# First couple's scores in two parts, joined sums and a newly laid order in a kernel of attention, gated MLP and mixture attention

## The chip, the cores and the metric

One core of a Trainium2 chip runs the whole program. The metric is the device time of one execution in microseconds (us), the median of several runs. The engines are named TensorE (PE in the rows, PEld its weight loads), VectorE (DVE), ScalarE (ACT), GpSimd (POOL) and SyncE (SP, which issues DMAs).

## The reference

Three layers follow one another, on 4 batches of 576 positions and 512 channels.

```python
# first attention: 8 heads of 64, each position sees itself and the 63 before it
scores = scale * np.matmul(q, k.transpose(0, 1, 3, 2))
scores = np.where((rel >= 0) & (rel < 64), scores, -1e9)
attn = np.exp(scores - np.max(scores, axis=-1, keepdims=True))
attn = attn / (np.sum(attn, axis=-1, keepdims=True) + 1e-09)
x = attn @ v
# gated MLP
h = np.maximum(x @ w_in, 0.0); u, v = h[..., :512], h[..., 512:]
v_n = (v - mean(v)) / np.sqrt(var(v) + 1e-06)
x = (u * (np.einsum('ts,bsd->btd', w_spatial, v_n) + b_spatial)) @ w_out
# second attention: 4 experts, causal over 576 positions, the two best by x @ w_gate
for e in range(4):
    a = softmax(scale * (x @ wq[e]) @ (x @ wk[e]).T, causal)   # sum + 1e-09
    out += gate_weight[e] * (a @ (x @ wv[e]) @ wo[e])
```

## The kernel before

The three layers run as one stream of small pieces of work. Each piece is a node (a call of `N`, with the engine that does it, what it depends on, the buffers it takes and gives back). The table `ORDER` near the head of the file lists the nodes' numbers in the order in which their instructions are written out, and the string `ON` the engine of each node that may go to several (0 PE, 1 ACT, 2 DVE, 3 POOL, 4 SP). So the order on every engine is fixed when the program is built; an engine works through its own queue in that order and waits only where a semaphore makes it. Class `Planner`, whose method `start` keeps a clock for each engine, holds the rules by which such a table is found; its `CLASH` (VectorE against GpSimd) and `cold` (TensorE after a pause) are part of it. None of the planner runs on the chip.

The work falls into three stages that overlap.

*First attention* (`a_couple`, about 0 to 110 us). A group is a pair of heads with 192 query positions; two groups make a couple, and 24 couples are worked one after another. For a couple, TensorE computes 12 score blocks of 64 queries by 128 keys into two PSUM banks, one for each head of the pairs (`s_mm`, issued by the helper at L400); VectorE adds the mask, takes the row's bound and writes SBUF (`s_top`, L647, three instructions for each bank, each with a short one that reads its accumulator); ScalarE takes the exponential and the row sum (`s_exp`, L654, three for each bank); VectorE adds the prepared 1e-9 and takes the reciprocal (L673 and L675 on a tile `mx` for each bank); one of POOL, DVE and ACT scales (`s_norm`, L663); TensorE transposes (L681); and a copy `pt` (L411 on ACT, L415 on DVE) makes the operand of the product with v. The couples from `N_DT` = 16 on ("far") are transposed by VectorE (L702) and through DRAM instead; there both banks share one tile `mp`, with one reduction and one reciprocal (L698, L700).

The first two couples (n0 = 0 and 2) read their q and k from one load each, `kq`, of 768 columns. Ahead of the first scores TensorE multiplies a tile of zeros, `hot`: `WARM` such matmuls in one node, and single ones that the order puts where it likes.

*Gated MLP* (about 20 to 260 us). Weights and x are split into a high and a low part (names ending in h and l), and each product is three matmuls. TensorE's matmuls `bank<-xh,w`, `bank<-w,xl`, `bank<-wsp_h,vh` belong here. Copies and subtractions that make the parts are the helpers at L411, L413, L415 (copy on ACT, POOL, DVE) and L424 (subtract).

*Second attention* (about 240 to the end). `c_qk` and `c_v` make q, k and v of two experts at a time, `c_gate` the gate, `far`, `far4` and `unit` the scores, exponentials, sums plus 1e-9 and scaling (L1641 to L1656, L1686 to L1699, L1725 to L1732), `c_pv` the product with v, `c_wo` the output product, whose copies `ot` SyncE stores. A block of output is 128 positions by 512 columns; for the last batch's second block it is two halves of 256.

The lines that matter most:

```python
    a = N((PE, 427.0 * WARM), lambda e: heat(WARM), alloc=[warm], prio=-1e9)      # L518
    dve.tensor_tensor_reduce(out=at(j, e2), in0=sq(ps[:, j * 128:(j + 1) * 128]),  # s_top
                             in1=sq(mask(j)), scale=-0.125, scalar=3.0e38,
                             op0=ALU.add, op1=ALU.min, accum_out=mx[:, j, 0:1])
    act.activation(at(j, e2), at(j, e2), AF.Exp, bias=mx[:, j, 0:1], scale=-1.0,   # s_exp
                   accum_out=mx[:, j, 1:2])
    dve.tensor_reduce(out=mx[:, :, 3], in_=mx[:, :, 1:3], axis=AX.X, op=ALU.add)   # L673
    dve.reciprocal(mx[:, :, 3], mx[:, :, 3])                                       # L675
```

Of the kernel before, what the change touches and what calls it, by code (L numbers as in the profile page):

```python
# [1926 lines left out]
```

## Time and profile before

| | |
|---|---|
| runs | 407.94, 409.22, 411.59 us; median 409.22 |
| profiled execution | 408.59 us, of which the span of the trace is 406.8 |
| TensorE busy | 390.8 us (96%), granted clock 0.998 on average |
| VectorE, ScalarE, GpSimd busy | 333.2, 208.8, 209.9 us |
| moved by DMA | 72.45 MB |

The times are those of one core. The span runs from the first to the last instruction of the trace; durations and stretches below count from its start. TensorE's matmuls overlap in their records, so that a full stretch shows as all busy. A matmul in full 32-bit precision leaves two records.

### The profile page before, as it was taken

The page shows a single profiled execution, that of the slowest core. Times are in us where ns is not written, and L with a number is a line of the kernel's source. Part 1 is how long each engine was busy: PE and PEld are TensorE (multiplying, and loading weights), DVE is VectorE, ACT ScalarE, POOL GpSimd, SP SyncE. Part 2 cuts the span into 40 slices and gives each one's busy share as a digit, 9 for nine tenths or more (in the row PEclk, how much of TensorE's full clock was granted, in tenths as well). Part 3 has the DMA queues.
Part 4 walks back from the last instruction along what each step waited for, and adds up shares of the span by engine and source line. Part 5 has one row for each costly group of instructions (what it writes and reads, how often), then busy time and mean ns, then how long its engine had stood idle before and what let it go on. Part 6 is the DMA issues. An engine that isn't in the chain of part 4 may idle for free.

```text
span 406.8 us, 10676 instructions
## 1 busy us (share of the span) xinstructions
PE 390.8 (96%) x3678; PEld 346.3 (85%) x3678; DVE 333.2 (82%) x1213; ACT 208.8 (51%) x708; POOL 209.9 (52%) x278
## 2 busy tenths in 40 slices
PE   8798898999999999999999999999899989999996
PEld 7676688998799989998999999999689968896765
DVE  5998799879889868758747685899999999998852
ACT  4999786955296574321222141483573346354332
POOL 7787697455279545526371765355742255122400
PEclk9999999999999999999999999999999999999999
DMA  7999769679695855450220110028775977899874
GB/s 270 290 348 314 236 157 302 202 217 271 174 341 150 235 151 155 121 161 12 76 75 3 26 54 2 1 45 230 190 180 128 263 166 210 250 278 252 234 225 129
DMA packets 88410, 72.45 MB, mean 178 GB/s; under 512 B 15138, under 2 KB 80418, under 8 KB 88356
## 3 DMA queue, kind: packets, MB, share of 16 engines
q1 hardware_dynamic: 88356, 71.77, 61.3%
q8 instruction: 29, 0.48, 0.5%
q14 instruction: 25, 0.20, 0.1%
HBM read 47.89 MB, written 23.86 MB: 176 GB/s over the span
## 4 chain that ended last, share of the span: by engine, by line
PE 64%; DVE 23%; DMA 6%; ACT 3%; issue 3%; SPq 1%; POOL 0%; DVEq 0%; ACTq 0%
PE bank L400 63%; DVE p L1641 2%; DVE pa L647 2%; DVE p L1656 2%; DVE p L1686 2%; ACT pa L654 1%; DVE qk L424 1%; DMA qa<-in_qT_dram 1%; DMA d<-p 1%; SPq L506 1%; DMA pg<-d 1%; DMA kt<-in_kT_dram 1%; DMA dr<-pa 1%; DVE p L1653 1%; DVE pa L702 1%
## 5 line engine op out<-in xcount | busy, mean ns | idle before, releaser
L400 PE MATMUL bank<-xh,w 128*128 128x288 f32 x512 | 106.8, 296 | 0.4 <-DVE xl L424 0.4
L400 PEld LDWEIGHTS bank<-xh,w 128*128 128x128 f32 x512 | 83.5, 188 | 2.2 <-DVE xl L424 0.7
L400 PE MATMUL bank<-xl,w 128*128 128x288 f32 x256 | 75.4, 294 | 0.0
L400 PE MATMUL bank<-w,xh 128*128 128x512 f32 (+1 forms) x256 | 64.6, 342 | 0.1
L1653 POOL TENSOR_SCALAR p<-p,mg,fx 128x256 f32<-128x256 f32 (+3 forms) x45 | 27.7, 624 | 42.6 <-DVE ga L1539 10.0
L400 PEld LDWEIGHTS bank<-xl,w 128*128 128x128 f32 x256 | 48.1, 188 | 0.4
L400 PEld LDWEIGHTS bank<-w,xh 128*128 128x128 f32 x256 | 42.7, 188 | 5.2 <-ACT xh L411 0.3
L400 PE MATMUL bank<-w,xl 128*128 128x512 f32 (+1 forms) x128 | 43.3, 338 | 0.9 <-DVE xl L424 0.9
L1645 ACT ACTIVATE p<-p,mg 128x128 f32<-128x128 f32 (+3 forms) x56 | 30.9, 553 | 18.9 <-DVE mg L1641 10.6
L654 ACT ACTIVATE pa<-pa,mp 128x128 f32<-128x128 f32 x96 | 37.2, 391 | 2.2 <-issue 2.0
L647 DVE CUSTOM_DVE_ANT_0 pa<-bank,mask 128x128 f32<-128x128 f32 x120 | 28.4, 283 | 4.2 <-PE bank L400 4.1
L400 PE MATMUL bank<-qk 64*128 64x320 f32 (+4 forms) x288 | 27.7, 329 | 2.5 <-DVE qk L424 2.0
L400 PEld LDWEIGHTS bank<-qk 64*128 64x128 f32 x288 | 22.0, 185 | 6.8 <-ACT xh L411 1.8
L400 PEld LDWEIGHTS bank<-w,xl 128*128 128x128 f32 x128 | 24.1, 188 | 4.0 <-DVE xl L424 1.3
L1072 POOL TENSOR_TENSOR st<-st,nhalf 128x1 f32<-128x1 f32 (+1 forms) x20 | 14.2, 715 | 24.7 <-DVE st L1070 19.3
L1641 DVE CUSTOM_DVE_ANT_0 p<-bank,kmask 128x128 f32<-128x128 f32 (+3 forms) x56 | 25.1, 482 | 0.5
L424 POOL TENSOR_TENSOR vl<-vr,vh 128x512 fp32r<-128x512 f32 x14 | 19.2, 1374 | 11.0 <-ACT vh L411 10.7
L400 PE MATMUL bank<-pg,v 128*64 128x128 f32 (+2 forms) x224 | 23.9, 354 | 1.0 <-DVE qk L424 1.0
L400 PE MATMUL bank<-wsp_h,vh 128*128 128x288 f32 x80 | 24.0, 301 | 0.3 <-DVE mp L647 0.3
L400 PE MATMUL bank<-wsp_h,vl 128*128 128x288 f32 x80 | 23.6, 295 | 0.0
L400 PE MATMUL bank<-wsp_l,vh 128*128 128x288 f32 x80 | 23.6, 294 | 0.0
L1656 DVE STREAM_TRANSPOSE p<-p 128x768 f32<-128x768 f32 (+1 forms) x21 | 22.2, 1057 | 0.9 <-POOL p L1653 0.8
(277 smaller groups left out, 1053.6 us busy)
## 6 DMA issues: line engine op xcount, KB each, us to landing
vt<-in_v_dram SPq DMA_DIRECT2D x12, 512.0 KB, 5.8
dr<-pa SPq DMA_DIRECT2D x64, 96.0 KB, 3.1
pt<-dr SPq DMA_DIRECT2D x16, 384.0 KB, 4.7
d<-p SPq DMA_DIRECT2D x56, 96.0 KB, 2.0
qa<-in_qT_dram SPq DMA_DIRECT2D x44, 96.0 KB, 5.3
out_dram<-ot SPq DMA_DIRECT2D x15, 256.0 KB, 3.6
y<-in_w_in_dram SPq DMA_DIRECT2D x7, 512.0 KB, 6.3
d<-p SPq DMA_DIRECT2D x28, 128.0 KB, 3.0
```

Of the source, the lines that this page charges most:

```text
L400: pe.matmul(o, lhsT, rhs, start=start, stop=stop)
L424: engs[e].tensor_tensor(out=o, in0=a, in1=hi.bitcast(F32), op=ALU.subtract)
L506: nc.sync.dma_start(o, i)
L647: dve.tensor_tensor_reduce(out=at(j, e2), in0=sq(ps[:, j * 128:(j + 1) * 128]), in1=sq(mask(j)), scale=-0.125, scalar=3.0e38, op0=ALU.add, ...
L654: act.activation(at(j, e2), at(j, e2), AF.Exp, bias=mx[:, j, 0:1], scale=-1.0, accum_out=mx[:, j, 1:2])
L702: a = N((DVE, 902), lambda e: dve.transpose(pa.t, pa.t), [a], use=[pa], prio=prio, sbuf=True)
L1072: a = N((POOL, 560), lambda e: pool.tensor_tensor(out=st[:m, 9:10], in0=st[:m, 8:9], in1=nhalf[:m], op=ALU.pow), [n1], use=[st])
L1641: a = N((DVE, t_tt(L)), lambda _, ps=ps, c0=c0, L=L, I=I, e=e, n=n: dve.tensor_tensor_reduce(out=put(I, e), in0=as4(ps[:, c0:c0 + L]), in1 ...
L1645: done.append(N((ACT, 284 + 0.87 * L), lambda _, I=I, e=e, n=n: act.activation(put(I, e), put(I, e), AF.Exp, bias=mg[:, n, 0:1], scale=-1. ...
L1653: done.append(N({POOL: 328 + 0.832 * L, DVE: 190 + 0.52 * L}, lambda en, n=n, I=I, e=e: engs[en].tensor_scalar(put(I, e), put(I, e), mg[:, ...
L1656: a = N((DVE, 100 + 4.16 * w), lambda e: dve.transpose(P[:, :4 * w], P[:, :4 * w]), done, use=[P], prio=prio, sbuf=True)
L1686: dve.tensor_tensor_reduce(out=P[HALF[y], i * 320:(i + 1) * 320], in0=ps[y][HALF[y], :320], in1=tmask[HALF[y], 2 * i:2 * i + 2].rearrange( ...
```

## The change

- `kq`: the first couple's q and k are laid out anew in DRAM and loaded in two parts, 384 columns and 512; the second couple's load has 896 columns.
- The first couple's scores become two nodes: 4 matmuls (j = 0), which need only the first load, and 8 (j = 1, 2). `s_top` and `s_exp` are divided in the same way.
- Joined sums: the couples n0 = 4 to 14 use the shared tile `mp`, so that one reduction and one reciprocal (L716, L718 in the new numbering) serve both banks; both scalings depend on them.
- The tiles `mc` and `mg` of the second attention's sums are made once, set to 1e-9, and kept (nine memsets on POOL); the tensor_scalar that adds the constant stays, its result in another column for `mc`.
- `WARM` 7 to 5; in all there are 13 matmuls of `hot` in place of 18.
- Planner: a VectorE instruction on SBUF waits until GpSimd is free, and the reverse, in place of `CLASH`; pauses of TensorE add up to a debt; some costs are raised.
- `ORDER` and `ON` are replaced as a whole.

Among the engines of nodes, going by the counts before and after: `v` copies on VectorE 6 to 1, `pg` copies on VectorE 4 to 1, `qk` casts on VectorE 11 to 9, scalings of `p` on VectorE by `mg` 11 to 10, `wsp_l` subtractions on VectorE 0 to 2, `xl<-y,xh` subtractions on VectorE 0 to 2, 128x192 casts `xh` on VectorE 8 to 12 and `pt` copies on VectorE 1 to 2. One scaling of the first attention in three parts goes to ScalarE.

```diff
-WARM = 7
+WARM = 5
...
 ON = (
-    "00040440020220442404012201424441212110431244230222223232202243203410012412020421102320002244142132201241100220041222433123124314"
+    "00040004000220440414444444024204411222301224122042212341201221232412401012212202230323410120422124323011402022020222241013113244"
...
-    MX = [const.tile([128, 3, 4], F32, name=f"mx{i}") for i in range(6)]
+    MX = [const.tile([128, 3, 4], F32, name=f"mx{i}") for i in range(4)]
...
-    MP = [const.tile([128, 2, 3, 4], F32, name=f"mp{i}") for i in range(3)]
-    for x in MP:
+    MP = [const.tile([128, 2, 3, 4], F32, name=f"mp{i}") for i in range(4)]
+    MC = [const.tile([128, 6], F32, name=f"mc{i}") for i in range(4)]
+    MG = [const.tile([128, 4, 4], F32, name=f"mg{i}") for i in range(5)]
+    for x in MP + MC + MG:
         pool.memset(x, 1e-9)
...
-        Q_N[2 * x] = Q_N[2 * x + 1] = KV_N["kq", x] = load(128 * 3072, 1, lambda: dma(kq(x), kq0[x]), use=[KQ[x]], prio=prio)
+        KV_N["kq", x] = []
+        for cs in (slice(0, 384), slice(384, 896)) if x == 0 else (slice(0, 896),):
+            KV_N["kq", x].append(load(512 * (cs.stop - cs.start), 1, lambda cs=cs: dma(kq(x)[:, cs], kq0[x][:, cs]), use=[KQ[x]], prio=prio))
+        Q_N[2 * x] = Q_N[2 * x + 1] = KV_N["kq", x][-1]
...
+        if n0 == 0:
+            for js in ((0,), (1, 2)):
+                tops.append(N((PE, 60 + 210 * len(js)), lambda e, js=js: s_mm(e, js), kn[:1 if js[0] == 0 else None] + tops,
+                              alloc=[] if tops else bank, use=hk + (bank if tops else []), prio=prio, form=1))
+            top = tops[-1]
...
-        if far:
+        both = far or n0 >= 4
+        if both:
             mp = r_mp.new()
         for e2, ps in enumerate(bank):
-            mx = mp if far else r_mx.new()
+            mx = mp if both else r_mx.new()
...
+        if both:
+            a = N((DVE, 90), lambda e: dve.tensor_reduce(out=mp[:, :, :, 3], in_=mp[:, :, :, 1:3], axis=AX.X, op=ALU.add),
+                  done, use=[mp], prio=prio)
+            a = N((DVE, 116), lambda e: dve.reciprocal(mp[:, :, :, 3], mp[:, :, :, 3]), [a], use=[mp], prio=prio)
+            norms = [(a, mp, x) for x in norms]
...
-    r_mc = ring(p2, "mc", [128, 6], F32, 4)
-    r_mg = ring(p2, "mg", [128, 4, 4], F32, 5)
+    r_mc, r_mg = fixed(MC, False), fixed(MG, False)
```

The head of TensorE's queue before: `hot` are the fillers, `vt` holds the first couple's q and k, banks 69 and 70 take its scores.

```order
L400 MATMUL bank_68<-hot 128x128 x9
L400 MATMUL bank_69<-vt 64x128
L400 MATMUL bank_70<-vt 64x128
L400 MATMUL bank_69<-vt 64x128
L400 MATMUL bank_70<-vt 64x128
```

The same place after:

```order
L415 MATMUL bank_68<-hot 128x128 x11
L415 MATMUL bank_69<-vt 64x128
L415 MATMUL bank_70<-vt 64x128
L415 MATMUL bank_69<-vt 64x128
L415 MATMUL bank_70<-vt 64x128
```

Eleven fillers in place of nine stand ahead of the first scores. In the whole queue there were groups of 9, 2, 3 and 4 fillers; now there are groups of 11 and 2.

VectorE's queue before, in the first couples: `mx_92` and `mx_93` belong to the two banks of the first couple, `mx_94` to the second couple, `mx_96` and `mx_97` to the third (n0 = 4); ISA is the `s_top` instruction.

```order
L647 ISA pa,mx_95<-bank_72,mask_84 128x128
L647 ISA mx_95 128x1
L673 TENSOR_REDUCE mx_92<-mx_92 128x3
L675 RECIPROCAL mx_92<-mx_92 128x3
L647 ISA pa,mx_96<-bank_73,mask_84 128x128
L647 ISA mx_96 128x1
L647 ISA pa,mx_96<-bank_73,mask_84 128x128
L647 ISA mx_96 128x1
L647 ISA pa,mx_96<-bank_73,mask_84 128x128
L647 ISA mx_96 128x1
L673 TENSOR_REDUCE mx_93<-mx_93 128x3
```

After, from the last of the first couple's six subtractions on:

```order
L676 ISA pa,mx_93<-bank_70,mask_84 128x128
L676 ISA mx_93 128x1
L711 TENSOR_REDUCE mx_92<-mx_92 128x3
L713 RECIPROCAL mx_92<-mx_92 128x3
L676 ISA pa,mx_94<-bank_71,mask_83 128x128
L676 ISA mx_94 128x1
L676 ISA pa,mx_94<-bank_71,mask_84 128x128
L676 ISA mx_94 128x1
L676 ISA pa,mx_94<-bank_71,mask_84 128x128
L676 ISA mx_94 128x1
L711 TENSOR_REDUCE mx_93<-mx_93 128x3
L676 ISA pa,mx_95<-bank_72,mask_83 128x128
```

The first couple's reductions and its first reciprocal come before and between the second couple's subtractions, where they stood behind all of them. The third couple's sums before are an L673 and an L675 for each of `mx_96` and `mx_97`; after, they are one pair on `mp_100` for both banks, in this place:

```order
L871 SCALAR_TENSOR_TENSOR y_338<-bank_70,y_338 128x512
L716 TENSOR_REDUCE mp_100<-mp_100 128x6
L676 ISA pa,mp_101<-bank_68,mask_84 128x128
L676 ISA mp_101 128x1
L676 ISA pa,mp_101<-bank_68,mask_84 128x128
L676 ISA mp_101 128x1
L676 ISA pa,mp_101<-bank_68,mask_84 128x128
L676 ISA mp_101 128x1
L718 RECIPROCAL mp_100<-mp_100 128x6
```

Its reduction comes behind the subtractions of the next couple's first bank (`mp_101`).

The end of TensorE's queue before, the output product's last blocks:

```order
L400 MATMUL bank_75<-w,oh_3477 128x512 x2
L400 MATMUL bank_75<-w,ol_3483 128x512
L400 MATMUL bank_75<-w,oh_3478 128x512 x2
L400 MATMUL bank_75<-w,ol_3484 128x512
L400 MATMUL bank_68<-w,oh_3477 128x256 x2
L400 MATMUL bank_68<-w,ol_3483 128x256
L400 MATMUL bank_68<-w,oh_3478 128x256 x2
L400 MATMUL bank_68<-w,ol_3484 128x256
L400 MATMUL bank_69<-w,oh_3477 128x256 x2
L400 MATMUL bank_69<-w,ol_3483 128x256
L400 MATMUL bank_69<-w,oh_3478 128x256 x2
L400 MATMUL bank_69<-w,ol_3484 128x256
```

And after:

```order
L415 MATMUL bank_71<-w,oh_3470 128x256 x2
L415 MATMUL bank_71<-w,ol_3476 128x256
L415 MATMUL bank_71<-w,oh_3471 128x256 x2
L415 MATMUL bank_71<-w,ol_3477 128x256
L415 MATMUL bank_75<-w,oh_3470 128x512 x2
L415 MATMUL bank_75<-w,ol_3476 128x512
L415 MATMUL bank_75<-w,oh_3471 128x512 x2
L415 MATMUL bank_75<-w,ol_3477 128x512
L415 MATMUL bank_69<-w,oh_3470 128x512 x2
L415 MATMUL bank_69<-w,ol_3476 128x512
L415 MATMUL bank_69<-w,oh_3471 128x512 x2
L415 MATMUL bank_69<-w,ol_3477 128x512
```

The two halves of 256 columns stood last; now two blocks of 512 columns follow them, the last into bank 69. On ScalarE the last copy becomes `ot<-bank_69 128x512`, where it was `128x256`; on SyncE the last output becomes one of 256 columns from a buffer that two 64x512 outputs read just before.

## Rows read from the trace of the kernel before

**Rows 1.** The page: busy time, share and instructions of each engine

```profile
PE 390.8 (96%) x3678; PEld 346.3 (85%) x3678; DVE 333.2 (82%) x1213; ACT 208.8 (51%) x708; POOL 209.9 (52%) x278
```

**Rows 2.** Stretches: us, busy PE, PEld, DVE, ACT, POOL, PEclk, DMA share, GB/s

```profile
0.00:10.00 10.00, 8.56 (x100) 7.51 (x100) 5.09 (x38) 4.29 (x17) 7.16 (x37) 1.00 0.78 267
10.00:30.00 20.00, 17.28 (x272) 13.63 (x272) 19.73 (x115) 19.65 (x84) 16.49 (x20) 1.00 1.00 325
10.00:80.00 70.00, 62.68 (x815) 52.42 (x816) 63.19 (x293) 61.03 (x242) 51.77 (x54) 1.00 0.86 264
80.00:110.00 30.00, 30.00 (x344) 25.92 (x343) 25.94 (x93) 13.86 (x53) 13.79 (x14) 1.00 0.80 233
290.00:340.00 50.00, 46.57 (x392) 40.77 (x393) 47.66 (x178) 24.85 (x76) 22.27 (x29) 1.00 0.75 191
```

**Rows 3.** TensorE in time, from 1 us: start, us, what, idle before

```profile
1.05 4.21 PE L400 MATMUL bank<-hot 128*128 128x128 f32 x18 [1.05 <-DVE hot L432]
5.19 1.28 PE L400 MATMUL bank<-vt 64*64 64x128 f32 x24
...
7.86 0.94 PE L400 MATMUL bank<-hot 128*128 128x128 f32 x6
...
10.60 1.00 PE L400 MATMUL bank<-ut,qa 64*64 64x128 f32 x24 [0.99 <-DVE mx L673]
```

**Rows 4.** VectorE in time, its first score row

```profile
6.66 0.29 DVE L647 CUSTOM_DVE_ANT_0 pa<-bank,mask 128x128 f32<-128x128 f32 x1 [3.67 <-PE bank L400]
```

**Rows 5.** Groups of VectorE, 0 to 111: busy, mean ns, idle before

```profile
L675 DVE RECIPROCAL mx<-mx 128x3 f32<-128x3 f32 x16 | 2.8, 173 | 0.2
...
L673 DVE TENSOR_REDUCE mx<-mx 128x3 f32<-128x6 f32 x16 | 2.3, 151 | 0.0
L424 DVE TENSOR_TENSOR wol<-y,woh 128x576 fp32r<-128x576 f32 x1 | 2.1, 2053 | 0.0
...
L424 DVE TENSOR_TENSOR t2w<-y,t1w 64x576 fp32r<-64x576 f32 x1 | 0.7, 742 | 0.0
```

**Rows 6.** Groups of ScalarE, 10 to 60

```profile
L654 ACT ACTIVATE pa<-pa,mx 128x128 f32<-128x128 f32 x41 | 15.9, 398 | 0.0
...
L411 ACT ACTIVATE pt<-bank 128x384 f32<-128x384 f32 x15 | 6.7, 482 | 0.4 <-PE bank L681 0.3
...
L411 ACT ACTIVATE xh<-bank 128x192 fp32r<-128x192 f32 x10 | 3.0, 329 | 3.5 <-DVE xt L415 3.3
```

**Rows 7.** GpSimd and VectorE in time, near 286 us

```profile
286.20 1.42 POOL L424 TENSOR_TENSOR xl<-y,xh 128x576 fp32r<-128x576 f32 x1
...
286.25 1.47 DVE L1539 TENSOR_TENSOR ga<-lg 128x80 f32<-128x80 f32 x1
...
287.65 0.23 DVE L1540 TENSOR_TENSOR ga<-lg 128x80 f32<-128x80 f32 x1
```

**Rows 8.** Groups of VectorE, 240 to the end

```profile
L1653 DVE TENSOR_SCALAR p<-p,mg,fx 128x128 f32<-128x128 f32 (+3 forms) x11 | 5.7, 517 | 0.1
L415 DVE CAST qk<-bank 128x288 fp32r<-128x288 f32 x11 | 4.8, 439 | 1.7 <-PE bank L400 1.6
...
L415 DVE COPY v<-bank 128x256 f32<-128x256 f32 x6 | 2.5, 417 | 1.9 <-PE bank L400 1.8
...
L415 DVE COPY pg<-bank 128x512 f32<-128x512 f32 (+2 forms) x4 | 2.3, 584 | 1.1 <-PE bank L1741 1.1
```

**Rows 9.** What TensorE waited for: us in total, times, longest

```profile
PE bank L400 <- DVE qk L424: 3.0, 4, 1.4
```

**Rows 10.** ScalarE in time, at the end

```profile
399.80 0.60 ACT L411 ACTIVATE ot<-bank 128x512 f32<-128x512 f32 x1 [6.21 <-PE bank L400]
...
403.60 0.38 ACT L411 ACTIVATE ot<-bank 128x256 f32<-128x256 f32 x1 [0.37 <-PE bank L400]
```

**Rows 11.** DMA issues, 395 to 407: count, KB each, median us to landing

```profile
out_dram<-ot SPq DMA_DIRECT2D x3, 256.0 KB, 2.1
out_dram<-ot SPq DMA_DIRECT2D x4, 128.0 KB, 1.9
```

More of the change, by code (lines that the diff above doesn't have):

```diff
@@ L253, in start @@
         n.by = e
-        if e == PE and t - self.free[e] > 1500.0:
-            self.cold = t + 3400.0
-        self.free[e] = n.end = t + n.on[e]
-        if e == PE:
-            self.free[e] = n.end = n.end + self.DRAIN[self.form][n.form] + min(n.on[e], max(0.0, self.cold - t))
+        if e == POOL:
+            t = max(t, self.claim)
+        c, d = n.on[e], self.claimed
+        idle = max(0.0, t - self.free[e])
+        self.free[e] = n.end = t + c
+        if e == PE:
+            self.debt += idle
+            if idle > 1100.0 or self.debt > 1800.0:
+                self.cold, self.debt = t + 6000.0, 0.0
+            self.free[e] = n.end = n.end + self.DRAIN[self.form][n.form] + min(c, max(0.0, self.cold - t))
+            self.debt = max(0.0, self.debt - 0.5 * (n.end - t))
             self.form = n.form
         elif e == DVE:
+            self.claimed = None
             if n.sbuf:
-                self.free[e] = n.end = n.end + self.CLASH * max(0.0, self.free[POOL] - t)
-            self.sbuf = n.sbuf
-        elif e == POOL and self.sbuf:
-            self.free[e] = n.end = n.end + self.CLASH * max(0.0, self.free[DVE] - t)
+                self.claimed, self.claim, self.queued = n, t, -1.0
+                if self.free[POOL] > t:
+                    self.queued = self.free[POOL]
+                    self.free[e] = n.end = self.queued + c
+        elif e == POOL and d is not None and self.free[DVE] > t:
+            if self.queued >= 0.0 and t <= self.queued + 60.0:
+                self.queued = n.end
+                self.free[DVE] = d.end = n.end + d.on[DVE]
+                for s in d.use:
+                    s.free_at = max(s.free_at, d.end + self.LAT[DVE])
+            else:
+                self.free[e] = n.end = self.free[DVE] + c
         if e == SP:
@@ L622, in vap, with s_mm @@
             return hv[x][:, vi, c:c + 64]
-        def s_mm(_):
-            for j in range(3):
+        def s_mm(_, js=range(3)):
+            for j in js:
                 for x, e in ((0, 0), (1, 1), (1, 0), (0, 1)):
@@ L663, in s_norm @@
                     engs[e].tensor_tensor(out=o, in0=o, in1=mx[:, :, 3:4].to_broadcast([128, 3, 128]), op=ALU.mult)
[L665 to L670 removed]
+            own_ = both and e2 == 1
+            news = ([] if own_ else [mx]) + ([] if e2 else [pa])
+            if tops:
+                for js, t in zip(((0,), (1, 2)), tops):
+                    a = N((DVE, 210 * len(js)), lambda e, js=js, s_top=s_top: s_top(e, js=js), [t] + first, alloc=news,
+                          use=[ps] + ([] if news and not e2 else [pa]) + ([] if news else [mx]), prio=prio)
+                    news, first = [], [a]
+                    a = N((ACT, 390 * len(js)), lambda e, js=js, s_exp=s_exp: s_exp(e, js=js), [a], use=[pa, mx], prio=prio)
+            else:
+                a = N((DVE, 606), s_top, [top] + first, alloc=news, use=[ps] + ([mx] if own_ else []) + ([pa] if e2 else []), prio=prio)
+                first.append(a)
+                a = N((ACT, 1160), s_exp, [a], use=[pa, mx], prio=prio)
+            if both:
                 done.append(a)
+                norms.append(s_norm)
                 continue
@@ L1546, in c_gate @@
-        n2 = N_(150, lambda: tr_(out=rk(), in_=gt(), axis=AX.X, op=ALU.add), [n2])
-        n2 = N_(80, lambda: dve.tensor_scalar(rk(), rk(), 1.5, None, op0=ALU.is_lt), [n2])
-        n2 = N_(90, lambda: tt(out=ex.t, in0=ex.t, in1=rk(), op=ALU.mult), [n2, n4])
-        n2 = N_(90, lambda: tr_(out=m1(1), in_=ex.t, axis=AX.X, op=ALU.add), [n2])
-        n2 = N_(70, lambda: dve.tensor_scalar(m1(1), m1(1), 1e-9, None, op0=ALU.add), [n2])
-        n2 = N_(75, lambda: dve.reciprocal(m1(1), m1(1)), [n2])
@@ L1552, in c_gate @@
-        n4 = N_(90, lambda: tt(out=ex.t, in0=ex.t, in1=lead(1), op=ALU.mult), [n2])
-        n4 = N_(70, lambda: dve.tensor_copy(ex[HALF[1], 4, 0:NE:2], ex[HALF[1], 4, 1:NE:2]), [n4])
+        n2 = N_(270, lambda: tt(out=gt(), in0=gt(), in1=eq(), op=ALU.add), [n2, n3])
+        n2 = N_(260, lambda: tr_(out=rk(), in_=gt(), axis=AX.X, op=ALU.add), [n2])
+        n2 = N_(160, lambda: dve.tensor_scalar(rk(), rk(), 1.5, None, op0=ALU.is_lt), [n2])
+        n2 = N_(200, lambda: tt(out=ex.t, in0=ex.t, in1=rk(), op=ALU.mult), [n2, n4])
@@ L1554, in c_gate @@
+        n2 = N_(200, lambda: tr_(out=m1(1), in_=ex.t, axis=AX.X, op=ALU.add), [n2])
+        n2 = N_(160, lambda: dve.tensor_scalar(m1(1), m1(1), 1e-9, None, op0=ALU.add), [n2])
+        n2 = N_(160, lambda: dve.reciprocal(m1(1), m1(1)), [n2])
+        n4 = N_(200, lambda: tt(out=ex.t, in0=ex.t, in1=lead(1), op=ALU.mult), [n2])
+        n4 = N_(160, lambda: dve.tensor_copy(ex[HALF[1], 4, 0:NE:2], ex[HALF[1], 4, 1:NE:2]), [n4])
         n1 = nf
```

135 lines of the change are left out of this document (67 added, 68 removed), and 126 rows, old and new, of the table ORDER.

## Prediction

> **What bounds the kernel now.** I read the page first, then the stretches, then the order of instructions at the start, the groups of the stretches in which TensorE stands still, the table of what TensorE waits for, and the end.
>
> The busy line gives TensorE 390.8 of 406.8 us (96%) and VectorE 333.2 (82%) [rows 1]. TensorE bounds the whole, and a gain has to come out of its 16.0 us without work. The stretches say where these lie [rows 2]: 10 - 8.56 = 1.44 us in 0 to 10, 70 - 62.68 = 7.32 in 10 to 80, 50 - 46.57 = 3.43 in 290 to 340, while 80 to 110 has 30.00 of 30. In 10 to 30 both helpers are full (VectorE 19.73 of 20, ScalarE 19.65); in 290 to 340 only VectorE is (47.66 of 50, ScalarE 24.85). So the early pauses are shared by two engines, and the late ones belong to VectorE.
>
> A measurement of this kernel can tell about 1% from no change: its three runs spread from 407.94 to 411.59 us. Faster therefore means under 405.1 and slower over 413.3.
>
> **The start.** TensorE begins with nine filler matmuls, 18 records in 4.21 us from 1.05, or 0.234 us a record; the first couple's scores follow at 5.19, and their row names no wait [rows 3]. So the fillers ahead of them in the queue hold them, not the load. VectorE's first subtraction starts at 6.66, having waited 3.67 us for TensorE [rows 4]. The change loads the first third apart and lets VectorE begin after 4 of the couple's 12 matmuls. But the order still puts both parts behind the fillers, and these are now eleven. Two more cost 2 x 2 x 0.234 = 0.94 us, so the scores start near 6.1; VectorE gains at most two thirds of the 24 score records, 0.67 x 1.28 = 0.85 us. They cancel: 0, between -0.9 (the two fillers add nothing) and +0.9 (the split brings nothing).
>
> **Joined sums.** Six couples (4 to 14) have one reduction and one reciprocal in place of two each. These take 151 and 173 ns [rows 5], so six couples save 6 x 0.324 = 1.9 us of VectorE, if the wider forms cost what the narrow ones do. Against that, the first head's scaling now waits for the second head's three exponentials, 3 x 0.398 = 1.2 us a couple [rows 6], and TensorE's transposes stand behind that scaling. Other moved work eats the saving: four 128x192 casts (329 ns on ScalarE) and one 128x384 copy (482 ns) go from ScalarE to VectorE. By ScalarE's rows that is 4 x 0.329 + 0.482 = 1.8 us, and ScalarE takes over one scaling in three parts, which I set at 3 x 0.398 = 1.2 us [rows 6]. VectorE comes out even (-1.9 + 1.8), ScalarE 0.6 us lighter. By the amount of work alone the 7.32 us hardly shrink; what is left is the order: the second head's sum of the first couple is taken earlier, two later blocks of fillers are gone, and each helper's queue is laid out afresh. I take a quarter of the idle time: -1.8 us. Bounds: -5.5 (three quarters go) and +2.4 (two of the six couples show their 1.2 us).
>
> **VectorE's work of the middle.** Four subtractions of 128x576 with both inputs in SBUF (two for wsp_l, two for xl) come to VectorE. One of that shape took VectorE 2.053 us (wol), one of 64 rows and the same length 0.742 [rows 5]. Four cost 3.0 to 8.2 us of VectorE. Their cover is TensorE's dense run, 80 to 110 with 30.00 of 30 for one [rows 2], so I enter 0, and +2.0 for the range if one comes just where TensorE needs VectorE next. The spread has a reason in the trace: GpSimd began a 1.42 us subtraction at 286.20, and VectorE's 128x80 comparison at 286.25 took 1.47 us, the next of that size 0.23 [rows 7].
>
> [...]
>
> **The second attention.** Here VectorE loses work [rows 8]: five of six v copies at 0.417 (2.1 us), three of four pg copies at 0.584 (1.75), two of eleven qk casts at 0.439 (0.9), one of the eleven p scalings at 0.517 (0.5); the output and oh copies cancel but for some tenths. Sum -5.2 us. The constant added to the sums costs what it did, since it was a tensor_scalar before. ScalarE takes most of the copies and has 50 - 24.85 = 25 us free in 290 to 340 [rows 2]. TensorE waits for VectorE's qk subtractions 3.0 us in four waits, the longest 1.4 [rows 9], and idles 3.43 us there. The 5.2 us are spread over 160 us, and some lie behind the last of these waits; so I take 2.0 of the 3.43. Bounds: -3.4 (all of it) and +2.0 (ScalarE's longer queue makes the qk casts, and so the subtractions, late).
>
> **The end.** Before, the last block is 256 columns wide: its copy takes 0.38 us, a 512 wide one 0.60 [rows 10], and of the outputs the 128 KB ones land 1.9 us after issue, the 256 KB ones 2.1 [rows 11]. Now the last block is 512 wide: 0.22 + 0.2 = +0.4. Behind its output SyncE issues one more, of 256 columns, out of a buffer that two 64-row outputs have to leave first. For that I add 0.3. Together +0.7, between 0 and +1.9 (that output starts only when another has landed).
>
> **Sum.** 0 - 1.8 + 0 - 2.0 + 0.7 = -3.1 us. The profiled execution took 408.59 us (its span is 406.8): 405.5. The median of the runs shown lies 0.63 higher, which gives 406.1. I put the forecast between them, at 405.7; the likeliest case's own range is 402.5 to 409.
>
> **Rivals.**
> *The pauses only move.* A new order shortens the pauses one sees and opens others where TensorE is dense today only because the helpers happen to be ahead. For it: VectorE and ScalarE together have no less to do before 80. Against: VectorE has 5.2 us less after 240. Then only the end counts: 408.6 + 0.7 = 409.3.
>
> *Most pauses go.* Beyond the start 7.32 + 3.43 = 10.75 us are idle. If the order now spares VectorE the waits behind GpSimd (1.47 us in place of 0.23), three quarters may go: 408.6 - 8.1 + 0.7 = 401.2. Against: ScalarE is full in 10 to 30 [rows 2] whatever the order.
>
> *Slower: TensorE runs at half speed after the first couple.* Before, blocks of two, three and four fillers stand among the first couples' scores; of these only the two are left. The rows show that idling has a price at the start: a filler record takes 0.234 us from 1.05 on and 0.94 / 6 = 0.157 at 7.86; 24 score records take 1.28 us at 5.19 and 1.00 at 10.60 [rows 3]. [...] If TensorE works at half speed in half of 10 to 30, 8.64 us of its 17.28 are doubled, and the idle 2.72 / 2 soak up 1.4: 405.7 + 8.6 - 1.4 = 412.9; in all of the stretch it is near 420. It decides once 3.1 + 1.4 = 4.5 us of work are doubled, for then the gain is gone. For it: the 1.2 us waits for joined sums fall in this stretch. Against: a pause of 0.99 us ahead of 10.60 left those 24 records at 1.00 [rows 3].
> [...]
>
> **How the numbers follow.** Forecast 0.47, of which 0.22 fall under 405.1 and 0.25 within 1%. The pauses only move: 0.22 (0.17 within, 0.05 slower). Most pauses go: 0.17, faster. Half speed: 0.14, slower. That makes faster 0.39, same 0.42, slower 0.19. The bounds do not all fall on one side at once, so the range takes them in part: down to 400.0, which holds most of the second rival, up to 412.8, where the half-speed case begins. About 0.06 is left out below and 0.13 above.
>
> **What would show it.** Right: the first scores near 6.1 and VectorE's first subtraction still between 6.3 and 7.0; TensorE's idle time in 10 to 80 near 5.5 us and in 290 to 340 near 1.4; VectorE some 5 us less busy after 240; a last copy of 0.60 us on ScalarE and an output issued behind it. Wrong: VectorE starting a microsecond sooner; 24 score records taking over 1.2 us after 10 (half speed); idle time of TensorE between 110 and 260; transposes that wait over 1 us for the joined sums in several couples.

## The result and the profile after

The changed kernel takes 413.06 us (median of 9 runs, 411.53 to 414.80), the kernel before 409.70 beside it (9 runs, 407.94 to 411.59): a ratio of 1.0079, with a 95% interval of 1.0052 to 1.0105. It is slower by 0.8%, and 7.4 us above the forecast of 405.7. The profiled execution took 412.33 us; its span of 410.6 is 3.8 above the 406.8 of before.

The busy line of the page answers to [rows 1]:

```profile
PE 390.9 (95%) x3668; PEld 346.6 (84%) x3668; DVE 336.6 (82%) x1211; ACT 208.2 (51%) x707; POOL 204.5 (50%) x279
```

TensorE has the same 390.9 us of work as before (390.8), so the 3.8 us are, but for 0.1, time in which TensorE stands still. Where they arose is read from the stretches, as in [rows 2] (us, busy PE, PEld, DVE, ACT, POOL, PEclk, DMA share, GB/s). The kernel after:

```profile
0.00:10.00 10.00, 8.14 (x98) 7.25 (x98) 4.77 (x31) 3.92 (x15) 7.48 (x45) 1.00 0.82 256
10.00:20.00 10.00, 7.79 (x111) 5.90 (x111) 9.46 (x58) 9.53 (x44) 5.46 (x8) 0.83 0.98 305
10.00:80.00 70.00, 62.19 (x830) 51.75 (x834) 66.30 (x293) 61.90 (x243) 49.18 (x51) 0.98 0.87 261
80.00:260.00 180.00, 175.85 (x1579) 163.76 (x1572) 140.39 (x421) 67.99 (x228) 92.18 (x108) 1.00 0.46 131
260.00:400.00 140.00, 138.28 (x1138) 118.66 (x1138) 123.38 (x467) 72.55 (x221) 55.69 (x77) 1.00 0.70 189
400.00:410.60 10.60, 6.48 (x34) 5.18 (x33) 1.78 (x4) 1.79 (x3) 0.00 (x0) 0.91 0.54 168
```

The kernel before, in the stretches that [rows 2] do not have:

```profile
80.00:260.00 180.00, 179.56 (x1630) 167.87 (x1630) 138.98 (x426) 73.26 (x238) 94.57 (x107) 1.00 0.44 128
260.00:400.00 140.00, 136.48 (x1113) 115.59 (x1113) 125.48 (x459) 68.04 (x210) 56.37 (x81) 1.00 0.72 194
400.00:406.80 6.80, 3.51 (x28) 2.89 (x24) 0.42 (x1) 2.14 (x5) 0.00 (x0) 0.90 0.50 170
```

A stretch's length less TensorE's busy time is its idle time. The difference of the two kernels stands beside the terms of the forecast:

| stretch | idle before | idle after | difference | term of the forecast |
|---|---|---|---|---|
| 0 to 10 | 1.44 | 1.86 | +0.4 | start: 0 |
| 10 to 80 | 7.32 | 7.81 | +0.5 | joined sums and order: -1.8 |
| 80 to 260 | 0.44 | 4.15 | +3.7 | VectorE's work of the middle: 0 |
| 260 to 400 | 3.52 | 1.72 | -1.8 | second attention: -2.0 |
| 400 to the end | 3.29 | 4.12 | +0.8 | end: +0.7 |

The sum is +3.6, which with 0.1 of TensorE's work is the 3.8 of the spans but for rounding. The terms miss by 0.4 + 2.3 + 3.7 + 0.2 + 0.1 = 6.7 us of the 7.4; the rest is the median of the runs, 0.7 above the profiled execution. Two lines went as forecast, and one that stood at zero decides.

The runs below that share an order in a stretch show how far one trace speaks. In 80 to 260 TensorE idles 0.00 to 0.44 us with the order of before (before, h1, h2, p, c_all, j) and 2.96 to 5.20 with that of the change (after, e1 to e5, w1), so this line is clear. In 260 to 400 it is 3.2 to 3.7 with the order of before and 1.7 to 2.9 with that of the change. In 10 to 80 the two overlap (before, h1, h2, q, m885, m628: 6.60 to 7.47; after, e1 to e5: 6.78 to 8.33): the +0.5 says only that the 1.8 us were not gained.

What TensorE does at the start answers to [rows 3 and 4]; the last row is VectorE's first score row (start, duration):

```profile
1.05 4.98 PE L415 MATMUL bank<-hot 128*128 128x128 f32 x22 [1.05 <-DVE hot L447]
5.96 0.89 PE L415 MATMUL bank<-vt 64*64 64x128 f32 x24
...
7.02 0.29 DVE L676 CUSTOM_DVE_ANT_0 pa<-bank,mask 128x128 f32<-128x128 f32 x1 [3.71 <-PE bank L415]
...
15.72 1.81 PE L415 MATMUL bank<-ut,qa 64*64 64x128 f32 x24 [0.76 <-ACT pt L426]
```

The first scores come 0.77 us later (5.96 for 5.19; in the other traces of the same start between 5.13 and 6.04). VectorE began 1.06 us behind their start in place of 1.47, but this is not the split: the 24 score records took 0.89 us in place of 1.28, and VectorE still began only behind the last of them, 0.17 us after it (7.02 - 5.96 - 0.89) for 0.19 before (6.66 - 5.19 - 1.28). In every trace of a run with the split code this gap is 0.16 to 0.19 us. So the split gained nothing that a trace shows; what VectorE waits for beyond its 4 matmuls stays open. At 15.72 another 24 score records of the same shape take 1.81 us, about twice the 0.89 at 5.96: the half speed of the third rival, for a short stretch (the granted clock is 1.00 in 10 to 16, 0.52 in 16 to 18, 0.63 in 18 to 20, which makes the 0.83 of 10 to 20, and 1.00 again from 20 to 25).

### The profile page after: what moved, and what is told of

It reads as the page before. It is cut to its first block, busy times and chain, and to the rows that moved or that the text cites. A ratio compares the mean times of both kernels' runs of the same rounds, so it can differ in the third digit from the quotient of the medians.

```text
span 410.6 us, 10670 instructions
## 1 busy us (share of the span) xinstructions
PE 390.9 (95%) x3668; PEld 346.6 (84%) x3668; DVE 336.6 (82%) x1211; ACT 208.2 (51%) x707; POOL 204.5 (50%) x279
## 4 chain that ended last, share of the span: by engine, by line
PE 39%; DVE 15%; DMA 5%; issue 2%; ACT 2%; SPq 2%; POOL 1%; DVEq 0%; POOLq 0%
PE bank L415 38%; DMA pg<-d 3%; DVE p L1683 2%; SPq L523 2%; DVE p L1698 2%; DMA d<-p 1%; DVE p L1728 1%; DVE qk L439 1%; DVE mg L1690 1%; DVE st L1111 1%; PE bank L1783 1%; DVE pa L745 1%; ACT p L1687 1%; DVE y L868 1%; DMA out_dram<-ot 1%
## 5 line engine op out<-in xcount | busy, mean ns | idle before, releaser
L1695 POOL TENSOR_SCALAR p<-p,mg,fx 128x128 f32<-128x128 f32 (+3 forms) x46 | 28.0, 617 | 49.9 <-ACT qk L426 20.4
L683 ACT ACTIVATE pa<-pa,mp 128x128 f32<-128x128 f32 x132 | 51.1, 391 | 1.6 <-DVE mp L676 1.6
L1687 ACT ACTIVATE p<-p,mg 128x384 f32<-128x384 f32 (+3 forms) x56 | 31.0, 554 | 23.1 <-DMA d<-p 8.5
L415 PE MATMUL bank<-qk 64*128 64x320 f32 (+4 forms) x288 | 28.6, 331 | 1.2 <-DVE qk L439 0.6
L1683 DVE CUSTOM_DVE_ANT_0 p<-bank,kmask 128x384 f32<-128x384 f32 (+3 forms) x56 | 25.6, 480 | 1.1 <-PE bank L415 0.9
L439 POOL TENSOR_TENSOR vl<-vr,vh 128x512 fp32r<-128x512 f32 x14 | 19.6, 1407 | 11.8 <-DVE vh L430 8.4
L683 ACT ACTIVATION_READ_ACCUMULATOR pa<-pa,mp 128x1 f32 x132 | 25.1, 190 | 0.0
L1115 POOL TENSOR_TENSOR st<-st,nhalf 128x1 f32<-128x1 f32 (+1 forms) x20 | 12.9, 651 | 21.1 <-DVE st L1113 20.2
```

The lines of the kernel that those rows point to most:

```text
L415: pe.matmul(o, lhsT, rhs, start=start, stop=stop)
L439: engs[e].tensor_tensor(out=o, in0=a, in1=hi.bitcast(F32), op=ALU.subtract)
L1115: a = N((POOL, 680), lambda e: pool.tensor_tensor(out=st[:m, 9:10], in0=st[:m, 8:9], in1=nhalf[:m], op=ALU.pow), [n1], use=[st])
L1683: a = N((DVE, t_tt(L)), lambda _, ps=ps, c0=c0, L=L, I=I, e=e, n=n: dve.tensor_tensor_reduce(out=put(I, e), in0=as4(ps[:, c0:c0 + L]), in1 ...
L1687: done.append(N((ACT, 284 + 0.87 * L), lambda _, I=I, e=e, n=n: act.activation(put(I, e), put(I, e), AF.Exp, bias=mg[:, n, 0:1], scale=-1. ...
L1695: done.append(N({POOL: 328 + 0.832 * L, DVE: 190 + 0.52 * L}, lambda en, n=n, I=I, e=e: engs[en].tensor_scalar(put(I, e), put(I, e), mg[:, ...
```

## The experiments

Each hybrid keeps one program's code; a node is a line of `ORDER`, and its digit in `ON` is the engine.

### Which part of the program loses: three joins

h1 is the kernel before, with its nodes of second attention in the changed kernel's order and engines; q keeps the start and second attention of before and takes only what lies between; p is the reverse of q for the first phase, in the changed code.

```diff
 # h1: order of before to the end of the first phase, then
-ORDER, ON of before for second attention
+ORDER, ON of after for second attention
 # q: 477 nodes of before (about 72 us), then
-the rest of the first phase as before
+the rest of the first phase as after
 # p: 426 nodes of after (about 72 us), then
-the rest of the first phase as after
+the rest of the first phase as before
```

> The kernel before with the changed kernel's order and engines for the second attention alone (its 840 nodes are the same in both). By the two profiles the second attention takes 165.7 us from the last matmul of the gated MLP to the last matmul in the kernel before and 164.1 in the changed one, and the end takes 3.6 and 4.5 us: 409.7 - 1.6 + 0.9 = 409.0. Theory 'new pauses in the middle' has all of the loss before 240 and so expects 408.3 to 409.7. A theory that puts the loss into the second attention or its engines expects 411 or more.

> The kernel before with its own order to its first 477 nodes (about 72 us), then the changed kernel's order and engines for the rest of the first phase; second attention as before. Theory 'the order of the middle is what costs': 409.7 + 4.2 - 0.5 = 413.4 us (412 to 414.5), pauses in 100 to 180 us. Rival 'a backlog from the first 72 us': about 409.7 (409 to 410.5), since the start is the one of before.

> The changed kernel's code and its own order up to the first spatial matmul (its first 426 nodes, about 72 us), then the kernel before's order and engines for the rest of the first phase; second attention as changed. Theory 'the changed order of the middle is what costs' : the 4.2 us that the last matmul of the gMLP came later are gone, 409 us (408.3 to 410), and the idle TensorE of 80 to 260 us is again about 0.5 us. Rival 'the first 72 us leave VectorE and ScalarE with a backlog that shows only in the middle': still 412 to 413.5, with pauses in 100 to 180 us.

h1: 408.36 us (ratio 0.9974, 0.9950 to 0.9997), as expected: the new order of second attention is a small gain by itself. q: 415.80 (1.0151, 1.0121 to 1.0181). Its pauses of TensorE between 100 and 180 us (the brackets: idle before, and for whom) stand where those of the changed kernel stand. TensorE in time in the kernel after:

```profile
106.66 0.98 PE L415 MATMUL bank<-kt,qa 64*64 64x128 f32 x24 [0.48 <-DVE mp L676]
108.67 0.37 PE L415 MATMUL bank<-wsp_h,vh 128*128 128x288 f32 x1 [1.03 <-DVE mp L676]
138.54 0.37 PE L415 MATMUL bank<-wsp_h,vh 128*128 128x288 f32 x1 [0.48 <-ACT ut L434]
...
150.03 0.41 PE L415 MATMUL bank<-wsp_h,vh 128*128 128x288 f32 x1 [0.42 <-DVE y L871]
171.04 0.40 PE L415 MATMUL bank<-xh,w 128*128 128x288 f32 x1 [1.72 <-DVE xt L439]
```

The run q:

```profile
109.40 0.37 PE L400 MATMUL bank<-wsp_h,vh 128*128 128x288 f32 x1 [1.98 <-DVE mp L647]
139.25 0.37 PE L400 MATMUL bank<-wsp_h,vh 128*128 128x288 f32 x1 [0.49 <-ACT ut L419]
150.75 0.40 PE L400 MATMUL bank<-wsp_h,vh 128*128 128x288 f32 x1 [0.40 <-DVE y L828]
...
171.66 0.40 PE L400 MATMUL bank<-xh,w 128*128 128x288 f32 x1 [1.69 <-DVE xt L424]
```

The pauses of 0.48, 0.42 and 1.72 come back as 0.49, 0.40 and 1.69 behind a start that is not theirs. So they belong to the new middle, and the rival (a backlog from the first 72 us) falls. The time is 2.4 us above what was expected. In its trace the span is 6.3 us longer than before: 4.7 are idle time in 80 to 260, which is what the theory said, and 1.5 are longer work of TensorE (392.3 us busy, with 0.95 and 0.88 of the clock granted in 290 to 300 and 300 to 310).

p: 415.01 (1.0125, 1.0093 to 1.0156), a miss. In it 80 to 260 has no idle time at all, which the theory asked for, but the joint made one pause of 5.85 us at 77.18 us (for a `qa` load) and TensorE idles 20 - 13.57 = 6.43 us in 60 to 80 where the changed kernel has 2.01. Its row of 80 to 260:

```profile
80.00:260.00 180.00, 180.00 (x1629) 168.15 (x1628) 136.67 (x413) 73.37 (x241) 93.94 (x107) 1.00 0.45 128
```

Its time therefore says nothing on the middle; its trace agrees with q.

### One wait at a time

At 106 us VectorE's next score row stands still 2.36 us for ScalarE (a tile that a cast of `woh` still reads); at 171 TensorE waits 1.72 us for a subtraction `xt` queued late on VectorE. e1 moves the cast ahead, e2 the subtraction, e3 both and a relu `ut` at 138 us. (The expectations give the same pauses about 0.2 us longer than the brackets do.)

```diff
 # ORDER; e1: first pair, e2: second, e3: all three
-    779, 813, 161, 618,
+    562, 162, 161, 164,
-    912, 864, 825, 896,
+    831, 956, 825, 855,
-    644, 173, 709, 174,
+    900, 170, 709, 950,
```

> The changed kernel, one ScalarE copy (woh out of the raw tile pa) put eleven places of work earlier, ahead of the xh copy and the vr relu that wait for TensorE. Theory 'new pauses in the middle' (TensorE stands still 0.68 us at 106.65 and 1.24 us at 108.66 because VectorE's first score instruction of a couple waits until 105.84 for that copy to give the tile back): both pauses go, -1.6 us, 411.5. Rival 'the early clock' (TensorE at half speed between 15.7 and 19.5 makes the loss): no change, 413.1. Rival 'pauses only move': the two pauses go and others of about the same length open before 240, 413.

> The changed kernel, one VectorE subtraction (xt, 128x64) put ahead of a normalisation that waits for GpSimd. Theory 'new pauses in the middle' (TensorE stands still 1.90 us at 171.04 for a bank that this subtraction reads; ahead of it VectorE waits 1.94 us for GpSimd and then takes 1.49 us for the normalisation): that pause goes, -1.7 us, 411.4. Rival 'the early clock': no change, 413.1. Rival 'pauses only move': 413.

> Both moves and a third (a ScalarE relu of ut ahead of two couples' exponentials, for the pause of 0.66 us at 138.53). Theory 'new pauses in the middle': they add up, -1.6 -1.7 -0.5 = -3.8 us, 409.3, as fast as the kernel before. Rival 'the early clock': 413.1. Rival 'pauses only move': less than half of the sum, 411.5 or more.

412.59 (1.0082, 1.0053 to 1.0110), 412.50 (1.0072, 1.0045 to 1.0099) and 413.13 us (1.0081, 1.0052 to 1.0111): none differs from the changed kernel. In e2 the pause at 171 of 1.72 us became two, 0.34 at 172.26 and 1.07 at 173.86; in e3 that of 138 came back at 143.98 (0.51). In e1 the score row did start 2.36 us sooner, at 103.52 for 105.88, but VectorE's next piece then met GpSimd. The kernel after, and then e1:

```profile
106.52 0.70 DVE L439 TENSOR_TENSOR vl<-vr,vh 128x512 fp32r<-128x512 f32 x1
```

```profile
105.09 1.42 POOL L439 TENSOR_TENSOR wsp_l<-y,wsp_h 128x576 fp32r<-128x576 f32 x1
105.16 1.90 DVE L439 TENSOR_TENSOR vl<-vr,vh 128x512 fp32r<-128x512 f32 x1 [0.92 <-POOL vh L428]
...
108.50 0.37 PE L415 MATMUL bank<-wsp_h,vh 128*128 128x288 f32 x1 [1.71 <-DVE mp L676]
```

The subtraction waits 0.92 us for GpSimd and takes 1.90 in place of 0.70, ending 0.55 behind GpSimd's: what the move won is spent there, and TensorE pauses 1.71 us at 108.50 for 0.48 and 1.03. Moving the wait that ends last does not help while what stands behind it is as late. e1 to e3 keep 80 to 260 at 5.20, 3.81 and 3.88 us of idle time (4.15 in the changed kernel).

### The start, with its fillers back

```diff
 # ORDER: ten more single fillers
+    3, 11, 12,  ahead of 204 (first transposes of the first couple)
+    19, 21, 30, ahead of 207 (second transposes)
+    32, 35, 48, 49, behind 207
```

> The changed kernel with ten more of its filler matmuls (3 before the first transposes of the first couple, 3 before the second, 4 behind them), where TensorE stood still at 9.4, 13.9 and 15.0 us. Theory 'the half-speed stretch at 16 to 20 us (granted clock 0.52 and 0.63) is part of the loss': the granted clock of 10 to 20 us is 0.97 or more and the time falls by 1 to 2 us, to 411.0 to 412.0. Rival 'ScalarE and VectorE are the late ones there, and the loss is made later': 413.06 +- 0.6, whatever the clock.

414.26 us (1.0110, 1.0076 to 1.0145). The granted clock in 10 to 20 is 1.00 and TensorE idles 0.44 us there for 2.21, yet nothing is won. As a test of the clock the run is weak: e2 and e4 have the start of the changed kernel without these fillers, and their traces show 1.00 in 10 to 20 too. Nor is the pause of 0.94 us that its trace has at 93.83 a price of the fillers: e1 has one of 0.89 there, e5 one of 0.93.

What the clock is worth is better read from its mean in each execution, which is on record. Of 86 executions of the kernel before beside the experiments (one of 949 us left out), the 23 with a mean of 0.998 or more average 407.9 us, the other 63 410.0. Of the nine of the changed kernel the four with 0.998 or more average 412.3, the other five 413.5. At either clock the change loses, by 4.4 and 3.4 us, so half speed does not make the loss. But an execution at a lower clock is 1 to 2 us longer in both kernels; which of the two brings the other about is not shown.

### The code without its order

c_all has all the code of the change in the order and engines of before (a node waits for what it depends on, so the first head's scaling is moved behind the joined sum). j is the same with the sums of couples 4 to 14 for each head again.

```diff
 # c_all: ORDER, ON, WARM of before, mapped node by node
 # j, beside that (and six tiles mx for four):
-        both = far or n0 >= 4
+        both = far
```

> All the code of the change (first couple's scores in two parts, joined sums for couples 4 to 14, the constant written by tensor_scalar, the new tiles), with the kernel before's order, engines and warm-up matmuls for both phases. Theory 'the order costs, the code does not': 409.7 +- 0.8 us. Rival 'the code itself costs (joined sums hold the first half's weights back)': 411 or more, with the loss before 72 us. If the joined sums gave what the prediction credited to them: 408 or less.

> As the run with all the code of the change in the order of before, but couples 4 to 14 keep their sums for each half (the first couple still in two parts, the constant by tensor_scalar). Theory 'joined sums hold the first half's weights back, and in the old order TensorE waits for them (two pauses of 1.8 and 1.5 us at 42 and 44 us on GpSimd's weighting)': those pauses go and the time falls by 2.5 to 4 us, to 411.7 to 413.2. Rival 'the split of the first couple is what costs in that order': 415 or more, with the pauses of 10 to 20 us (3.5 us) alone.

c_all 415.73 (1.0148, 1.0112 to 1.0183), j 413.20 (1.0092, 1.0056 to 1.0128). So the code by itself, in the old order, is dearer than before, and 2.5 us of that are the joined sums, as the second expectation had it (the intervals overlap a little; TensorE's idle time in 10 to 80, 10.80 us in c_all and 8.24 in j, agrees). The rows of c_all in time show the way: the first of two scalings on GpSimd, which begins at 36.11 in the kernel before and at 36.01 in j, waits here until the joined reciprocal is done; the second follows behind a `w` subtraction, and TensorE's transposes wait for each. (The bracket of 4.88 names ScalarE's `vr`, which ended at 41.23, the reciprocal at 41.12; that it is the reciprocal is shown by j.)

```profile
40.93 0.19 DVE L718 RECIPROCAL mp<-mp 128x6 f32<-128x6 f32 x1
41.30 0.83 POOL L693 TENSOR_TENSOR pa<-pa,mp 128x384 f32<-128x384 f32 x1 [4.88 <-ACT vr L434]
...
42.18 0.55 PE L727 MATMUL bank<-ident,pa 128*128 128x128 f32 x3 [1.77 <-POOL pa L693]
...
44.20 0.84 PE L727 MATMUL bank<-ident,pa 128*128 128x128 f32 x3 [1.47 <-POOL pa L693]
```

In j both pauses are gone. The new order of the first 72 us has mainly made good what the new code costs there (7.81 us idle in 10 to 80 in the changed kernel). What the remaining 4.0 us of j are (413.20 for 409.20 of before beside it) was not separated; part is the mapped start (2.82 us idle in 10 to 20 for 2.34).

### Order and engines exchanged singly

x1 keeps the new order and gives 113 pieces of the middle the engine of before, x2 the reverse (109 pieces).

```diff
 # x1: ON behind 72 us, first phase    # x2: the same in the kernel before
-engine of after                       -engine of before
+engine of before                      +engine of after
```

> The changed kernel's order, with the kernel before's choice of engine for the 113 copies, splits and weightings after 72 us that the change gives to another engine. Theory 'the middle is late because work went from ScalarE to VectorE' (in 120 to 260 us VectorE 103.3 to 107.2 us, ScalarE 50.2 to 42.9): the four pauses of 106 to 173 us shrink below 1 us in all and the time is 409 to 410. Rival 'the order of the instructions makes the pauses, whoever runs them': pauses of 3 us or more stay in 100 to 180 us, 412 or more.

> The kernel before and its order, with the changed kernel's choice of engine for the same pieces after 72 us (109 of them). Theory 'the engines': 412 to 414, pauses in 100 to 180 us. Rival 'the order': 409.7 to 411, idle TensorE of 80 to 260 us below 1.5 us.

416.24 (1.0170, 1.0139 to 1.0201) and 421.35 us (1.0298, 1.0265 to 1.0331). Both are worse than either kernel, with pauses of their own (6.6 and 8.8 us idle in 80 to 260). Neither theory is borne out: an order fits its own engines only, and this pair does not tell which of the two is at fault.

### Where in the middle

Both join the kernel before (with the second attention of h2, below, 407.03 us) to the new order at a later point.

```diff
 # m885: 885 nodes of before (about 170 us), then
 # m628: 628 nodes of before (about 110 us), then
-the rest of the first phase as before
+the rest of the first phase as after
```

> The kernel before with the second attention and end that reached 407.0, but from its 886th listed node on (about 170 us) to the end of the first phase in the changed kernel's order and engines. Theory 'all that the middle loses is lost before 175 us, where the pauses are': 407.0 +- 0.8. Rival 'the order behind 175 us costs too': 408.5 or more.

> The same, but the changed kernel's order and engines already from the 629th node on (about 110 to 120 us). Theory 'each pause costs by itself, where it stands': what lies behind the seam is the pauses of 120 to 173 us (0.5, 0.4, 1.7), so 409.6 (408.8 to 410.4). Rival 'it is one lateness that begins before 110 us and is only shown later': 407.0 to 408. A seam may add a pause of its own at 110 to 120 us; it is then taken off.

m885: 409.19 us (0.9980, 0.9958 to 1.0002). Its only pause of 1.49 us stands at the joint (173.27, for a subtraction `t1v`); without it 407.7, within 0.7 of 407.03. m628: 412.55 (1.0069, 1.0046 to 1.0092), with 2.16 us at the joint (115.86) and behind it 0.47, 0.42 and 1.72: the sizes of the changed kernel once more. Without the joint 410.4, near the 409.6 of the theory that each pause costs by itself, and far from the rival's 408. So the loss is made before 175 us, pause by pause.

### VectorE beside GpSimd

This is what GpSimd and VectorE do ahead of the pauses of 150 and 171 us in the kernel after (start, duration):

```profile
146.74 1.72 POOL L742 TENSOR_TENSOR pa<-pa,mp 128x768 f32<-128x768 f32 x1
147.09 1.91 DVE L868 SCALAR_TENSOR_TENSOR y<-y,y 128x512 int32<-128x512 int32 x1
...
168.84 1.27 POOL L1042 TENSOR_TENSOR vr<-vr 128x512 f32<-128x512 f32 x1
168.90 1.49 DVE L1117 TENSOR_SCALAR vr<-vr,st 128x512 f32<-128x512 f32 x1 [1.94 <-POOL st L1115]
...
170.77 0.22 DVE L439 TENSOR_TENSOR xt<-bank,xt 128x64 fp32r<-128x64 f32 x1
170.85 1.29 POOL L439 TENSOR_TENSOR vl<-vr,vh 128x512 fp32r<-128x512 f32 x1 [0.74 <-DVE vh L430]
170.90 1.78 DVE L439 TENSOR_TENSOR vl<-vr,vh 128x512 fp32r<-128x512 f32 x1
```

Three VectorE instructions that begin 0.05 to 0.35 us behind one of GpSimd end 0.28 to 0.54 us behind its end. e4 takes two of GpSimd's pieces away and leaves the order alone; e5 adds the three moves of e3.

```diff
 # ON, nodes 927 (weighting, L742) and 866 (subtraction, L1042)
-POOL, POOL
+ACT, DVE
```

> The changed kernel with two pieces taken off GpSimd where VectorE's instructions beside them lasted 1.91 and 1.49 us instead of about 0.7: the weighting of 146.7 us goes to ScalarE, the subtraction of 168.8 us to VectorE. Theory 'VectorE's longer instructions beside GpSimd make the pauses of 147 to 173 us': 1.2 and 0.8 us of VectorE's time go, pauses of 140 to 180 us from 2.1 to 0.7 or less, 411.6 or less. Rival 'only the waits' order': pauses stay, 413 +- 0.6.

> The three moved waits of the earlier run (413.1) and the two pieces taken off GpSimd, together. Theory 'waits and lengthened instructions hold each other up, so that only both together help': pauses of 100 to 180 us from 4.8 to 2 or less, 410 to 411. Rival 'the queues are late as a whole and the pause goes where the next wait is': 412.5 to 413.5.

e4: 411.04 us (1.0032, 1.0003 to 1.0060), e5: 410.59 (1.0029, 1.0008 to 1.0050). e4 is some 2 us below the changed kernel and within the 411.6 or less of its theory. The same VectorE instructions in e4, with TensorE's pause:

```profile
147.57 0.69 DVE L868 SCALAR_TENSOR_TENSOR y<-y,y 128x512 int32<-128x512 int32 x1
...
168.06 0.55 DVE L1117 TENSOR_SCALAR vr<-vr,st 128x512 f32<-128x512 f32 x1 [1.93 <-POOL st L1115]
...
169.11 0.68 DVE L1042 TENSOR_TENSOR vr<-vr 128x512 f32<-128x512 f32 x1
169.25 0.40 PE L415 MATMUL bank<-xh,w 128*128 128x288 f32 x1 [0.30 <-DVE xt L439]
169.71 0.68 DVE L439 TENSOR_TENSOR vl<-vr,vh 128x512 fp32r<-128x512 f32 x1
```

1.91 became 0.69, 1.49 became 0.55, 1.78 became 0.68, although VectorE has one piece of 0.68 more; the pause at 150 is gone and that at 171 is 0.30 (169.25 us). The changed kernel's interval (from 1.0052) and that of e4 (to 1.0060) hardly overlap, and the trace names the rows, so this is taken as shown: VectorE held up by GpSimd makes the pauses of 150 and 171 us, 2.14 us that became 0.30, and with them a third to a half of the middle's loss. (TensorE's idle time in 80 to 260 fell only from 4.15 to 180 - 177.04 = 2.96, since its trace has a pause of 0.64 us at 93.80, the place that w1, e1 and e5 have one at and e4 did not touch; the medians differ by 2.0.) e5 is not told from e4. Its pause of 1.69 us at 108.56 stands behind the same `vl` row as in e1, 1.90 us beside GpSimd's `wsp_l`, which e5 left on GpSimd: by the rows the pauses of 106 to 109 have VectorE beside GpSimd as a second cause behind the wait for `woh`, and taking that piece away too was not tried. The pause of 138 us is one of 0.50 at 145.35 there; what makes it is open.

### A version that beats both

h2 is h1 with the last blocks in the order of before: the two of 256 columns at the very end.

```diff
 # last output blocks on TensorE (batch 3)
-t=3, t=1 left half, t=4, t=1 right half, t=0, t=2
+t=4, t=3, t=2, t=0, t=1 right half, t=1 left half
```

> The kernel before's first phase and the changed kernel's order of second attention, but its last blocks in the order of before, with the two blocks of 256 columns at the very end and each copy issued behind its block. Theory 'the 256-column blocks at the end shorten the way from the last matmul to the end': from the last matmul to the end of the span 3.6 us instead of 4.5, and 407.5 us (406.8 to 408.2), which would beat both kernels. Rival 'the end is set by the output queue': 408.4 as in the run without it.

407.03 us (0.9950, 0.9928 to 0.9973) against the 409.20 of before beside it and the 413.06 of the change. It beats before clearly; from h1 (0.9950 to 0.9997) its interval does not part it. From the start of TensorE's last record to the end of the span it is 405.2 - 401.6 = 3.6 us, as expected; in the changed kernel it is 410.6 - 406.08 = 4.5.

## Why the prediction was wrong, and where it was right

**The failed step is the term for the middle, entered at 0.** The step read: TensorE's dense run, 30.00 of 30 in 80 to 110 [rows 2], is the cover for what comes to VectorE, with +2.0 at the most. It measured +3.7, and no run with the whole new middle has less than 2.5 us more than before there. The dense run was taken for a reserve; it was the outcome of an order in which the helpers are just in time, and the runs q, m628 and m885 show that another order of the same pieces opens pauses there whatever precedes it. The four subtractions that the step priced at 3.0 to 8.2 us took the lower bound, and none stands ahead of a pause (they run at 65, 66 and 251 us). Their groups in the kernel after:

```profile
L439 DVE TENSOR_TENSOR wsp_l<-y,wsp_h 128x576 fp32r<-128x576 f32 x2 | 1.5, 744 | 0.0
L439 DVE TENSOR_TENSOR xl<-y,xh 128x576 fp32r<-128x576 f32 x2 | 1.4, 742 | 0.0
```

What the step read from [rows 7], a VectorE instruction lengthened beside one of GpSimd, came again; its place was not the one named: other instructions met GpSimd (1.91, 1.49 and 1.78 us beside it, 0.69, 0.55 and 0.68 in e4), and e4 prices them at 1.2 to 2.0 us. In the rows of 105 to 171 us VectorE's instructions end 0.28 to 0.55 us behind GpSimd's; what this was worth here is shown by e4 alone.

**Joined sums and the early order, -1.8, measured +0.5.** This is the second step that failed: the quarter of the idle time that was to go had no row under it. The sums saved what the step said (reduction 155 ns and reciprocal 184 wide, for 151 and 173 narrow [rows 5]), but VectorE came out even only over 0 to 110 us (94.5 us busy, 94.2 before); in 10 to 80 it is 3.1 us busier, 66.30 for 63.19 [rows 2]; the bound on the other side, first-head scalings held up, is what c_all shows and j takes back. (In the order shown ahead it is the reciprocal of `mp_100`, not its reduction, that stands behind the next couple's subtractions.)

**Second attention, -2.0, measured -1.8** (between 0.3 and 2.0 by the ranges above). Of the 5.2 us that were to leave VectorE 3.1 did: it is busy 139.58 us from 240 to the end before, and 136.46 from 244.5 to the end after, with 1296 TensorE records in either. In the table of waits of the kernel after, TensorE's wait for the subtractions `qk` answers to [rows 9] (3.0 us in four waits, the longest 1.4):

```profile
PE bank L415 <- DVE qk L439: 0.6, 1, 0.6
```

h1 has this part alone, and the time falls by 0.3%, with the interval just clear of none.

**The end, +0.7, measured +0.8.** The last copies in the kernel after, in time, answer to [rows 10]: a 512 wide copy, and behind it one more output of 256 columns whose copy waited for a DMA.

```profile
406.51 0.60 ACT L426 ACTIVATE ot<-bank 128x512 f32<-128x512 f32 x1 [0.74 <-PE bank L415]
406.80 0.42 DVE L430 COPY ot<-bank 128x256 f32<-128x256 f32 x1 [3.02 <-DMA out_dram<-ot]
```

**The start, 0, measured +0.4**, within its bounds, but not as reckoned: the scores came 0.77 us later, as the fillers' price had it, and the split, entered at up to 0.85, gave nothing. That VectorE came only 0.36 us later (7.02 for 6.66) is luck: the score records were shorter, 0.89 us for 1.28.

**The rivals.** "The pauses only move" had the mechanism and too low a price, since it held their sum fixed (409.3): they moved into a stretch that had none, while those it left at the start stayed. "Half speed" came near in time (412.9) for another reason: it holds for about 4 us in this trace (0.52 granted in 16 to 18, 0.63 in 18 to 20), e2 and e4 do without it, and at a full clock the change loses as much. The half was an assumption, which no row of before shows. Idling alone does not bring it on: TensorE idles 2.58 and 2.15 us of 10 to 20 in e2 and e4 with 1.00 granted, 2.21 in the changed kernel with 0.83. Behind p's pause of 5.85 us 24 score records took 1.68 us, for 0.89 at 67.01, with 0.85 granted in 60 to 80.
